# Splitting the first weight loads by use, k ahead of q in tiles 0 and 1, and w1, w3, w2 in more pieces

## The chip, the cores and the metric

One core of one Trainium2 chip runs the whole program. The metric is the device time of one execution in microseconds; the median of the runs counts.

## What is computed

A gated mix of a linear-attention block (a) and a gated feed-forward block (b), both of the same x (2048 tokens of 512, bf16). The reference, cut:

```
g = sigmoid((x * gate_w).sum(-1))
# a: 32 heads of 16
q, k, v = split(x @ wqkv)
pq, pk = phi(q), phi(k)          # phi(t) = where(t > 0, t + 1, exp(t)) + 1e-6
kv = einsum("bhsd,bhse->bhde", pk, v);  z = sum over s of pk
a = (pq @ kv) / (pq @ z + 1e-6) @ wo
# b: F = 1376
b = (silu(x @ w1) * (x @ w3)) @ w2
out = g * a + (1 - g) * b
```

## The kernel before

Tokens are cut into 16 tiles of 128 (`NT`), the model width 512 into four parts of 128 (`KC`, the index `kc`). The order of work on every engine is the order in which the program writes it; there is no planner. All loads are issued by one queue, SP's (`dq = nc.sync`), except for a small one (`touch`) on ACT's. Each DMA takes the next of eight semaphores in turn, and so an issue waits until the DMA eight places before it has landed.

**Loads** (L120 to L160). `x_first` brings the first two tiles of x into `xN` in natural layout. Then `load_wqk(kc)` (L126) brings four quarters of 256 KB, each with the rows of one kc and the columns of both q and k: `wqk[:, kc, :]`, of which `wq` is the first half of the columns and `wk` the second. After them come the DMA transposes that fill `xT` (x with the width on the partitions) for tiles 2 to 15 (L123), mixed with the natural loads of further tiles (L141), then the remainder columns `wr`, and the feed-forward weights `w1`, `w3` (one DMA each, L150), `wv`, `wo`, `w2` (one DMA, L154) and `w2x`.

**The first stage** (L372 to L419). Thirteen matmuls on a constant run while the loads are under way (L359). Tiles 0 and 1 of x are transposed by matmuls with an identity (L365) into PSUM banks, and copied to `xT` by DVE and ACT in turn (L379 to L382, L394). The projections of tiles 0 and 1, four accumulations (k and q of two tiles), go in the order of kc for the first two quarters, with k and q side by side (L183); then k's last two quarters, then q's. `phi` takes a finished accumulation through ACT's Exp (L196) and two DVE operations (L198, L201). `g_step(t)` multiplies xN's tile with pk's tile into the four banks 0 to 3, one for each kc, over all 16 tiles (L231). Banks 4 to 7 are handed out in turn by `mm_tile()`. Since `k_step(2)` takes bank 3 for its projection, the g_steps of tiles 0 and 1 do three banks first and the fourth later. From tile 2 on, each round of the loop is q of tile t, k of tile t + 2, g of tile t.

**Later stages.** The sum of pk over the tokens (`zacc`, on GpSimd), kv folded with wv and wo into `M2`, then for four blocks of 512 tokens the feed-forward (`glu_step`, L303 and L309), and for each tile the output (`out_step`, L475 and L492).

Of the kernel before, what the change touches and what calls it, by code (L numbers as in the profile page):

```python
# [8 lines left out]
ACT = mybir.ActivationFunctionType  # L9
# [7 lines left out]
def kernel(  # L17
# [17 lines left out]
    nc = tc.nc  # L35
    P = nc.NUM_PARTITIONS

    Bb, S, D = A_x.shape
# [3 lines left out]
    KC = D // P  # L42
    NT = S // P
# [3 lines left out]
    FC = F // P  # L47
# [14 lines left out]
    wqkv_r = A_wqkv.rearrange("(kc d) n -> d kc n", d=P)  # L62
    w1_r = B_w1.rearrange("(kc d) f -> d kc f", d=P)
    w3_r = B_w3.rearrange("(kc d) f -> d kc f", d=P)
# [15 lines left out]
        out=bmask[:], in_=bmask[:], pattern=[[-Dh, HPC], [0, Dh]], compare_op=ALU.is_ge,  # L80
# [3 lines left out]
        out=bmask[:], in_=bmask[:], pattern=[[Dh, HPC], [0, Dh]], compare_op=ALU.is_ge,  # L84
# [23 lines left out]
    wqk = consts.tile([P, KC, 2 * D], BF16, name="wqk")  # L108
    wq = wqk[:, :, 0:D]
    wk = wqk[:, :, D : 2 * D]  # L110
# [3 lines left out]
    w1 = consts.tile([P, KC, F0], BF16, name="w1")  # L114
    w3 = consts.tile([P, KC, F0], BF16, name="w3")
    w2 = consts.tile([P, FC, D], BF16, name="w2")
    xT = consts.tile([P, KC, S], BF16, name="xT")
    act_pre = consts.tile([P, 1], BF16, name="act_pre")
    dq = nc.sync
# [2 lines left out]
        ts = slice(t * P, (t + 1) * P)  # L122
        dq.dma_start(out=xT[:, :, ts], in_=x2d[ts, :], transpose=True)  # L123

    def load_wqk(kc):
        dq.dma_start(out=wqk[:, kc, :], in_=wqkv_r[:, kc, 0 : 2 * D])  # L126

    x_first = x2d[0 : 2 * P, :].rearrange("(p j) d -> p j d", j=2)
    dq.dma_start(out=xN[:, 0:2, :], in_=x_first)  # L129
# [1 line left out]

    touch = consts.tile([P, 2, 16], BF16, name="touch")
    nc.scalar.dma_start(out=touch[:], in_=wqkv_r[:, 1:3, 0:16])
    for kc in range(KC):
        load_wqk(kc)
    natural = {3: (2, 4), 5: (4, 8), 8: (8, 16)}
    for t in range(2, NT):
        load_xT(t)
# [3 lines left out]
    with nc.allow_non_contiguous_dma(reason="gate column"):  # L142
        dq.dma_start(
            out=wr[:, :, 2 * FR : NR], in_=gate_w.rearrange("(kc d o) -> d kc o", d=P, o=1)
        )
    dq.dma_start(out=wr[:, :, 0:FR], in_=w1_r[:, :, F0:F])
    dq.dma_start(out=wr[:, :, FR : 2 * FR], in_=w3_r[:, :, F0:F])
    for w, w_r, cuts in ((w1, w1_r, (0, KC)), (w3, w3_r, (0, KC))):
        for a, b in zip(cuts, cuts[1:]):
            dq.dma_start(out=w[:, a:b, :], in_=w_r[:, a:b, 0:F0])  # L150
    dq.dma_start(out=wv[:], in_=wqkv_r[:, :, 2 * D : 3 * D])
    dq.dma_start(out=wo[:], in_=A_wo.rearrange("(kc d) n -> d kc n", d=P))
    w2_r = B_w2[0:F0, :].rearrange("(fc f) d -> f fc d", f=P)
    dq.dma_start(out=w2[:], in_=w2_r)  # L154
    w2x_r = B_w2[F0:F, :].rearrange("(i r) d -> i (r d)", i=RP)
    dq.dma_start(
        out=w2x[:].rearrange("p r d -> p (r d)"),
        in_=w2x_r[None].to_broadcast([TPB, RP, RG * D]),
# [11 lines left out]
    bank = [psum.tile([P, D], FP32, name=f"bank{i}") for i in range(8)]  # L170
    turn = {"mm": 0, "ab": 0}

    def mm_tile():
        turn["mm"] += 1
        return bank[4 + (turn["mm"] - 1) % 4]
# [6 lines left out]
    def proj_mm(ps, t, w, kc):  # L182
        nc.tensor.matmul(  # L183
            ps[:], lhsT=xT[:, kc, t * P : (t + 1) * P], rhs=w[:, kc, :],
            start=(kc == 0), stop=(kc == KC - 1),
        )

    def project(t, w, ps=None):
        ps = mm_tile() if ps is None else ps
        for kc in range(KC):  # L190
            proj_mm(ps, t, w, kc)
        return ps

    def phi(ps, dst, name):
        e = work.tile([P, D], BF16, tag="e", bufs=4, name="e" + name)
        nc.scalar.activation(out=e[:], in_=ps[:], func=ACT.Exp)  # L196
        em = work.tile([P, D], BF16, tag="em", bufs=4, name="em" + name)
        nc.vector.tensor_scalar(  # L198
            out=em[:], in0=e[:], scalar1=1.0, scalar2=1e-6, op0=ALU.min, op1=ALU.add
        )  # L200
        nc.vector.scalar_tensor_tensor(  # L201
            out=dst, in0=ps[:], scalar=0.0, in1=em[:], op0=ALU.max, op1=ALU.add
        )
# [3 lines left out]
    def k_phi(t, ps):  # L207
        pk[t] = work.tile([P, D], BF16, tag="pk", bufs=5, name="pk")
        phi(ps, pk[t][:], "k")
        if t == 0:  # L210
            nc.gpsimd.tensor_copy(out=zacc[:], in_=pk[t][:])
        else:
            for i in range(ZP):
                cs = slice(i * D // ZP, (i + 1) * D // ZP)
                nc.gpsimd.tensor_tensor(  # L215
                    out=(zaccb if t == NT - 1 else zacc)[:, cs], in0=zacc[:, cs],
                    in1=pk[t][:, cs], op=ALU.add,
                )

    def k_step(t, ps=None):  # L220
        k_phi(t, project(t, wk, ps))

    def q_phi(t, ps):
        phi(ps, pq[:, t, :], "q")

    def q_step(t):
        q_phi(t, project(t, wq))

    def g_step(t, kcs=range(KC)):
        for kc in kcs:  # L230
            nc.tensor.matmul(  # L231
                bank[kc][:], lhsT=xN[:, t, kc * P : (kc + 1) * P], rhs=pk[t][:],
                start=(t == 0), stop=(t == NT - 1),
            )
# [128 lines left out]
    def transpose_block(t, kc, dst):  # L363

        nc.tensor.matmul(  # L365
            dst, lhsT=xN[:, t, kc * P : (kc + 1) * P], rhs=ident[:], start=True, stop=True
        )

    def transpose_kc(kc, ps):
        for t in range(2):  # L370
            transpose_block(t, kc, ps[:, t * P : (t + 1) * P])
# [3 lines left out]
    for t in range(2):  # L375
        transpose_block(t, 0, bank[t][:, 0:P])
    transpose_kc(1, bank[2])
    transpose_kc(2, bank[3])
    nc.vector.tensor_copy(out=xT[:, 0, 0:P], in_=bank[0][:, 0:P])  # L379
    nc.scalar.activation(out=xT[:, 0, P : 2 * P], in_=bank[1][:, 0:P], func=ACT.Copy)  # L380
    nc.vector.tensor_copy(out=xT[:, 1, 0 : 2 * P], in_=bank[2][:, 0 : 2 * P])
    nc.scalar.activation(out=xT[:, 2, 0 : 2 * P], in_=bank[3][:, 0 : 2 * P], func=ACT.Copy)  # L382
    first = {(t, n): mm_tile() for n, t in (("k", 0), ("k", 1), ("q", 0), ("q", 1))}
    w_of = {"k": wk, "q": wq}

    def first_mm(n, t, kc):
        proj_mm(first[t, n], t, w_of[n], kc)

    for kc in range(2):
        for n, t in (("k", 0), ("q", 0), ("k", 1), ("q", 1)):  # L390
            first_mm(n, t, kc)
        if kc == 0:
            transpose_kc(3, bank[0])
            nc.vector.tensor_copy(out=xT[:, 3, 0 : 2 * P], in_=bank[0][:, 0 : 2 * P])  # L394
    for kc in range(2, KC):
        for t in range(2):
            first_mm("k", t, kc)
    k_phi(0, first[0, "k"])
    k_phi(1, first[1, "k"])
    for kc in range(2, KC):  # L400
        first_mm("q", 0, kc)
    for kc in range(2, KC):
        first_mm("q", 1, kc)

    k_step(2, bank[3])
    q_phi(0, first[0, "q"])
    g_step(0, range(KC - 1))
    ps3 = project(3, wk)
    q_phi(1, first[1, "q"])
    k_phi(3, ps3)  # L410
    g_step(1, range(KC - 1))
    g_step(0, [KC - 1])
    g_step(1, [KC - 1])
    for t in range(2, NT):
        q_step(t)
        if t + 2 < NT:
            k_step(t + 2)
        g_step(t)


# [180 lines left out]
```

## Time and profile before

| | |
|---|---|
| median of 3 runs | 178.57 us (177.76 to 178.59) |
| the profiled execution | 178.0 us, of which 176.3 us span |
| granted TensorE clock | 1.0 |
| PE busy | 172.5 us, 98% of the span, 969 matmuls |
| DVE / ACT / POOL busy | 110.4 / 59.1 / 63.2 us |
| chain that ended last | PE 94%, DMA 2%, SP's queue 1% |
| HBM | 8.86 MB read, 2.10 MB written |
| DMA queue of SP | 28948 packets, 15.41 MB, 35.3% of 16 engines |

Times in the profile count from the start of the span. PE is TensorE's matmuls, PEld its weight loads, SPq SyncE's queue, which issues DMAs. A matmul's end is modelled, so that consecutive matmuls overlap in the records: what counts is the distance of their starts. The chain is followed back from the last instruction, at each step to what released it.

### The profile page before, as it was taken

Reading aid. Unit: us, or ns where it says so; the run is one execution under the profiler, and the core shown is the slowest. Engines: PE = TensorE matmul, PEld = TensorE weight load, DVE = VectorE, ACT = ScalarE, POOL = GpSimd, SP = SyncE. Lnnn points to the kernel's source line nnn. Section 1 sums busy time; section 2 is a strip of 40 time slices with the busy share of each in tenths; the row PEclk is TensorE's granted clock in tenths of the full one; section 3 lists DMA queues with packets and bytes.
Section 4 is the critical chain, followed back from the end, with each engine's and each line's share of the span. In section 5 each row is a group of like instructions: output and inputs, shape, how many; then the busy total and the mean of one; then the engine's idle time right before and its main releaser. Section 6 shows DMA issues by size and latency. Waiting matters only on the chain.

```text
span 176.3 us, 2685 instructions
## 1 busy us (share of the span) xinstructions
PE 172.5 (98%) x969; PEld 82.5 (47%) x969; DVE 110.4 (63%) x207; ACT 59.1 (34%) x109; POOL 63.2 (36%) x106
## 2 busy tenths in 40 slices
PE   8999999999999999999999999999999999999993
PEld 5444444444456443444444466444444444444453
DVE  1399788888764899777343477853435775344363
ACT  4354544544753443422423101134225123422000
POOL 5086657557300668486400044550000562000000
DMA  6998959995204111323200013330000233000001
GB/s 186 262 178 228 183 103 279 402 349 198 66 4 52 26 30 34 83 65 89 60 0 0 0 33 84 84 89 0 0 4 0 60 89 89 4 0 0 30 30 60
DMA packets 29232, 15.57 MB, mean 88 GB/s; under 512 B 21028, under 2 KB 27428, under 8 KB 29220
## 3 DMA queue, kind: packets, MB, share of 16 engines
q1 hardware_dynamic: 28948, 15.41, 35.3%
q8 instruction: 7, 0.11, 0.3%
q10 hardware_dynamic: 272, 0.01, 0.1%
q14 instruction: 5, 0.04, 0.1%
HBM read 8.86 MB, written 2.10 MB: 62 GB/s over the span
## 4 chain that ended last, share of the span: by engine, by line
PE 94%; DMA 2%; SPq 1%; DVE 0%; issue 0%
PE bank L492 20%; PE bank L303 20%; PE bank L309 20%; PE bank L183 15%; PE bank L231 8%; PE bank L475 8%; PE bank L245 3%; DMA wqk<-in_A_wqkv_dram 2%; PE bank L278 2%; SPq L126 1%; PE bank L447 0%; SPq L129 0%; PE bank L462 0%; DVE o L498 0%
## 5 line engine op out<-in xcount | busy, mean ns | idle before, releaser
L315 DVE TENSOR_TENSOR hT<-bank,sg 128x512 bf16<-128x512 f32 x40 | 27.3, 682 | 31.0 <-PE bank L309 30.9
L303 PE MATMUL bank<-xT,w 128*128 128x512 bf16 x160 | 41.1, 379 | 0.0
L309 PE MATMUL bank<-xT,w 128*128 128x512 bf16 x160 | 41.1, 379 | 0.0
L314 ACT ACTIVATE sg<-bank 128x512 bf16<-128x512 f32 x40 | 23.9, 597 | 45.9 <-PE bank L303 45.9
L492 PE MATMUL bank<-w,hT 128*128 128x512 bf16 (+2 forms) x180 | 37.5, 355 | 0.0
L337 POOL TENSOR_TENSOR pqs<-pq,rden 128x512 bf16<-128x512 bf16 x16 | 16.9, 1056 | 54.4 <-issue 46.9
L183 PE MATMUL bank<-wqk,xT 128*128 128x512 bf16 x128 | 30.8, 381 | 0.1
L215 POOL TENSOR_TENSOR zacc<-zacc,pk 128x128 f32<-128x128 f32 x56 | 23.3, 446 | 10.4 <-DVE pk L201 10.4
L492 PEld LDWEIGHTS <-hT 128*128 128x128 bf16 x180 | 16.7, 98 | 18.4 <-issue 0.8
L309 PEld LDWEIGHTS <-w 128*128 128x128 bf16 x160 | 15.7, 98 | 18.9
L303 PEld LDWEIGHTS <-w 128*128 128x128 bf16 x160 | 15.5, 98 | 18.2 <-issue 0.2
L498 DVE SCALAR_TENSOR_TENSOR o<-bank,omg_all,aga 128x512 bf16<-128x512 f32 (+2 forms) x18 | 12.5, 692 | 14.6 <-PE bank L492 11.7
L183 PEld LDWEIGHTS <-xT 128*128 128x128 bf16 x128 | 12.4, 98 | 15.2 <-issue 0.7
L322 POOL TENSOR_TENSOR pr<-pq,zb 128x512 f32<-128x512 bf16 x16 | 18.4, 1154 | 0.1
L231 PE MATMUL bank<-pk,xN 128*128 128x512 bf16 x64 | 16.4, 379 | 0.0
L475 PE MATMUL bank<-M,pqT 128*128 128x512 bf16 x64 | 16.1, 379 | 0.0
L196 ACT ACTIVATE eq<-bank 128x512 bf16<-128x512 f32 x16 | 9.4, 597 | 16.0 <-PE bank L183 16.0
L201 DVE SCALAR_TENSOR_TENSOR pk<-bank,emk 128x512 bf16<-128x512 f32 x16 | 11.1, 692 | 1.6
L196 ACT ACTIVATE ek<-bank 128x512 bf16<-128x512 f32 x16 | 9.4, 597 | 6.7 <-PE bank L183 6.7
L201 DVE SCALAR_TENSOR_TENSOR pq<-bank,emq 128x512 bf16<-128x512 f32 x16 | 11.1, 692 | 0.5
L326 DVE TENSOR_REDUCE den<-pr 128x32 f32<-128x512 f32 x16 | 10.8, 676 | 0.0
L231 PEld LDWEIGHTS <-xN 128*128 128x128 bf16 x64 | 6.3, 98 | 7.6
(54 smaller groups left out, 95.7 us busy)
## 6 DMA issues: line engine op xcount, KB each, us to landing
w<-in_B_w_dram SPq DMA_DIRECT2D x3, 1280.0 KB, 10.2
out_dram<-o SPq DMA_DIRECT2D x15, 128.0 KB, 1.9
wqk<-in_A_wqkv_dram SPq DMA_DIRECT2D x4, 256.0 KB, 3.7
xN<-in_A_x_dram SPq DMA_DIRECT2D x1, 1024.0 KB
xN<-in_A_x_dram SPq DMA_DIRECT2D x2, 256.0 KB, 2.8
xN<-in_A_x_dram SPq DMA_DIRECT2D x1, 512.0 KB, 4.7
wv<-in_A_wqkv_dram SPq DMA_DIRECT2D x1, 512.0 KB, 11.2
wo<-in_A_wo_dram SPq DMA_DIRECT2D x1, 512.0 KB, 12.1
```

What stands on the lines that cost most here:

```text
L183: nc.tensor.matmul(ps[:], lhsT=xT[:, kc, t * P : (t + 1) * P], rhs=w[:, kc, :], start=(kc == 0), stop=(kc == KC - 1),)
L196: nc.scalar.activation(out=e[:], in_=ps[:], func=ACT.Exp)
L201: nc.vector.scalar_tensor_tensor(out=dst, in0=ps[:], scalar=0.0, in1=em[:], op0=ALU.max, op1=ALU.add)
L215: nc.gpsimd.tensor_tensor(out=(zaccb if t == NT - 1 else zacc)[:, cs], in0=zacc[:, cs], in1=pk[t][:, cs], op=ALU.add,)
L231: nc.tensor.matmul(bank[kc][:], lhsT=xN[:, t, kc * P : (kc + 1) * P], rhs=pk[t][:], start=(t == 0), stop=(t == NT - 1),)
L303: nc.tensor.matmul(g_ps[:], lhsT=w1[:, kc, fs], rhs=xT[:, kc, tok], start=(kc == 0), stop=(kc == KC - 1),)
L309: nc.tensor.matmul(u_ps[:], lhsT=w3[:, kc, fs], rhs=xT[:, kc, tok], start=(kc == 0), stop=(kc == KC - 1),)
L314: nc.scalar.activation(out=sg[:], in_=g_ps[:], func=ACT.Silu)
L315: nc.vector.tensor_tensor(out=hT[tb][:, fc, :], in0=u_ps[:], in1=sg[:], op=ALU.mult)
L322: nc.gpsimd.tensor_tensor(out=pr[t][:], in0=pq[:, t, :], in1=zb[:], op=ALU.mult)
L475: nc.tensor.matmul(ps[:], lhsT=pqT[:, c, ts], rhs=M2[:, c, :], start=(c == 0), stop=(c == KC - 1),)
L492: nc.tensor.matmul(ps[:, 0 : cs.stop - cs.start], lhsT=hT[tb][:, fc, tt * P : (tt + 1) * P], rhs=w2[:, fc, cs], start=(fc == 0 and not sta ...
```

## The change

The first weights are loaded as wk quarter 0, wk quarter 1 (128 KB each), wk quarters 2 and 3 together, wq quarters 0 and 1 together, wq quarters 2 and 3 together (256 KB each): five DMAs in place of four. w1 and w3 are loaded in four DMAs each in place of one, w2 in two. In all that is eight DMAs more, 80 in place of 72.

The transposes of kc 2 and kc 3 of tiles 0 and 1 go between the projections: kc 2 behind k's first quarter and kc 3 behind its second. k of tiles 0 and 1 is finished in all four kc, then q, by halves. k_step(2) no longer uses bank 3 but the next bank of `mm_tile()`, and the g_steps of tiles 0 and 1 are whole. The loop now starts at tile 0.

```diff
-    def load_wqk(kc):
-        dq.dma_start(out=wqk[:, kc, :], in_=wqkv_r[:, kc, 0 : 2 * D])
+    def load_w(w, lo, hi):
+        cs = slice(D, 2 * D) if w is wk else slice(0, D)
+        dq.dma_start(out=w[:, lo:hi, :], in_=wqkv_r[:, lo:hi, cs])
...
-    for kc in range(KC):
-        load_wqk(kc)
+    for w, lo, hi in ((wk, 0, 1), (wk, 1, 2), (wk, 2, 4), (wq, 0, 2), (wq, 2, 4)):
+        load_w(w, lo, hi)
...
-    for w, w_r, cuts in ((w1, w1_r, (0, KC)), (w3, w3_r, (0, KC))):
+    for w, w_r, cuts in ((w1, w1_r, range(KC + 1)), (w3, w3_r, range(KC + 1))):
         for a, b in zip(cuts, cuts[1:]):
             dq.dma_start(out=w[:, a:b, :], in_=w_r[:, a:b, 0:F0])
...
-    dq.dma_start(out=w2[:], in_=w2_r)
+    for a, b in ((0, FC // 2), (FC // 2, FC)):
+        dq.dma_start(out=w2[:, a:b, :], in_=w2_r[:, a:b, :])
...
     transpose_kc(1, bank[2])
-    transpose_kc(2, bank[3])
     nc.vector.tensor_copy(out=xT[:, 0, 0:P], in_=bank[0][:, 0:P])
     nc.scalar.activation(out=xT[:, 0, P : 2 * P], in_=bank[1][:, 0:P], func=ACT.Copy)
     nc.vector.tensor_copy(out=xT[:, 1, 0 : 2 * P], in_=bank[2][:, 0 : 2 * P])
-    nc.scalar.activation(out=xT[:, 2, 0 : 2 * P], in_=bank[3][:, 0 : 2 * P], func=ACT.Copy)
-    first = {(t, n): mm_tile() for n, t in (("k", 0), ("k", 1), ("q", 0), ("q", 1))}
-    w_of = {"k": wk, "q": wq}
-
-    def first_mm(n, t, kc):
-        proj_mm(first[t, n], t, w_of[n], kc)
-
-    for kc in range(2):
-        for n, t in (("k", 0), ("q", 0), ("k", 1), ("q", 1)):
-            first_mm(n, t, kc)
+    ps_k = [mm_tile() for _ in range(2)]
+    for kc in range(KC):
+        for t in range(2):
+            proj_mm(ps_k[t], t, wk, kc)
         if kc == 0:
+            transpose_kc(2, bank[3])
+            nc.scalar.activation(
+                out=xT[:, 2, 0 : 2 * P], in_=bank[3][:, 0 : 2 * P], func=ACT.Copy
+            )
+        if kc == 1:
             transpose_kc(3, bank[0])
             nc.vector.tensor_copy(out=xT[:, 3, 0 : 2 * P], in_=bank[0][:, 0 : 2 * P])
-    for kc in range(2, KC):
+    k_phi(0, ps_k[0])
+    k_phi(1, ps_k[1])
+    ps_q = [mm_tile() for _ in range(2)]
+    for half in range(2):
         for t in range(2):
-            first_mm("k", t, kc)
-    k_phi(0, first[0, "k"])
-    k_phi(1, first[1, "k"])
-    for kc in range(2, KC):
-        first_mm("q", 0, kc)
-    for kc in range(2, KC):
-        first_mm("q", 1, kc)
-
-    k_step(2, bank[3])
-    q_phi(0, first[0, "q"])
-    g_step(0, range(KC - 1))
-    ps3 = project(3, wk)
-    q_phi(1, first[1, "q"])
-    k_phi(3, ps3)
-    g_step(1, range(KC - 1))
-    g_step(0, [KC - 1])
-    g_step(1, [KC - 1])
-    for t in range(2, NT):
-        q_step(t)
+            for kc in range(2 * half, 2 * half + 2):
+                proj_mm(ps_q[t], t, wq, kc)
+    q_phi(0, ps_q[0])
+    for t in range(NT):
+        if t > 1:
+            q_step(t)
         if t + 2 < NT:
             k_step(t + 2)
+        if t == 0:
+            q_phi(1, ps_q[1])
         g_step(t)
```

## The prediction, made before the changed kernel had run

> **What bounds the kernel now.** I read four views: the page's chain of work and busy times, the chain in order of time over the first 14 us, the timeline of the start, and the DMA answers for single loads. The page first.
>
> ```profile
> span 176.3 us, 2685 instructions
> PE 172.5 (98%) x969; PEld 82.5 (47%) x969; DVE 110.4 (63%) x207; ACT 59.1 (34%) x109; POOL 63.2 (36%) x106
> PE 94%; DMA 2%; SPq 1%; DVE 0%; issue 0%
> ```
>
> TensorE is the end-setter: 94% of the chain. The 2% of DMA is one piece, early. The chain over 0 to 14 us shows it:
>
> ```profile
> 1.25 0.42 SPq L126
> ...
> 2.66 4.38 DMA wqk<-in_A_wqkv_dram
> 7.04 0.04 issue
> 7.08 2.32 PE bank L183 x10
> 9.40 0.65 PE bank L231 x3
> ```
>
> The fourth quarter of wqk, issued at 2.66, lands at 7.04; the first matmul that needs it (k, kc 3, tile 0) starts at 7.08. From there the chain is PE without a break: ten matmuls in a row, then g_step, and so on to the end. I went through the starts of PE's matmuls after 7.08: a 512-column matmul follows another every 0.216 us, and what exceeds that is eight gaps of about 0.1 us, where the tiled matmuls of L278, L447 and L462 begin or end. The change touches none of these, so whatever it does to the time it does before about 13 us, while it delays no load past its use. The timeline there:
>
> ```profile
> 3.92 0.29 DVE L379 CAST xT<-bank 128x128 bf16<-128x128 f32 x1 [3.92 <-PE bank L365]
> 4.24 0.42 DVE L381 CAST xT<-bank 128x256 bf16<-128x256 f32 x1
> 4.26 1.26 PE L183 MATMUL bank<-wqk,xT 128*128 128x512 bf16 x4
> 4.45 0.38 ACT L382 ACTIVATE xT<-bank 128x256 bf16<-128x256 f32 x1
> 5.47 3.93 PE L183 MATMUL bank<-wqk,xT 128*128 128x512 bf16 x16
> 5.67 0.42 DVE L394 CAST xT<-bank 128x256 bf16<-128x256 f32 x1 [1.01 <-PE bank L365]
> 7.49 1.09 ACT L196 ACTIVATE ek<-bank 128x512 bf16<-128x512 f32 x2 [2.66 <-PE bank L183]
> 8.45 0.69 DVE L201 SCALAR_TENSOR_TENSOR pk<-bank,emk 128x512 bf16<-128x512 f32 x1
> 9.38 0.69 DVE L201 SCALAR_TENSOR_TENSOR pk<-bank,emk 128x512 bf16<-128x512 f32 x1
> ```
>
> The first projection matmul starts at 4.26, as soon as DVE's copy of xT (kc 0, tile 0) is done at 4.21. Ten of the sixteen matmuls of tiles 0 and 1 run before 7.08 and six after it: the sixteenth is done at 7.08 + 6 x 0.216 = 8.37, when k_step(2) begins. The only DMA wait in the whole PE stream is from 6.79 (the tenth, started at 6.58, has streamed) to 7.08: **0.29 us**.
>
> **The loads.** The four quarters of wqk (256 KB each, issued at 1.25, 1.72, 2.19 and 2.66) take 2.9, 3.2, 4.1 and 4.4 us, and so land at 4.12, 4.96, 6.32 and 7.04. After the change the same 1 MB goes as 128, 128, 256, 256 and 256 KB, k's half first. Two terms come with it. Rows of 2048 bytes become rows of 1024: in the trace's packet records a 2048-byte packet takes 84 ns and a 1024-byte one 46 ns, so each of the 16 DMA engines carries 64 x 46 = 2.94 us in place of 32 x 84 = 2.69, **+0.26 us** for the last byte. And SP issues one more DMA: 0.43 us (a wqk row) to 0.59 us (a two-row natural load). I count that at nothing for the weights, because the last quarter waits 4.4 us from issue with the engines busy all along; if that cover is gone it costs up to 0.59. By byte position: wk's first quarter about 3.8, its second about 4.2 to 4.5, its second half 4.96 + 0.13 = about 5.1, wq's first half 6.32 + 0.2 = 6.5, its second 7.04 + 0.3 = **7.35**. Bounds for the last: 6.9 (the last 2048-byte packet ends at 6.62, plus 0.26, no hold-up after it) to 8.9 (7.04 + 0.26 + 0.59 + one more stall like the longest packet of that stretch, 1.03). I take 7.35, nearest the quarter's own row.
>
> **PE's new order, step by step**, with the spacings of before (0.40 and 0.26 us for the two matmuls at 4.26 and 4.66, 0.216 later, 0.056 for a transpose). Four transposes in place of six run ahead of the copies; DVE's copy still ends at 4.21, so k kc 0 starts at 4.26 and 4.66. Transposes of kc 2 at 4.93, k kc 1 at 5.04 and 5.26, transposes of kc 3 at 5.47 and 5.53. k kc 2 could start at 5.58 but needs ACT's copy of the kc 2 block, which before lay hidden at 4.45: transpose done at 5.20, copy 0.38, about 5.68 (+0.10 new wait). k kc 3 needs DVE's copy: block done at 5.75, copy 0.42, 6.21 plus the 0.06 from copy to matmul: 6.26 and 6.48 (+0.15 new wait). So k of both tiles ends its stream at 6.69, and eight q matmuls follow: 6.69 + 8 x 0.2155 = **8.42**, if wq's first half is there by 6.65 (6.5 expected) and the second by 7.56 (7.35 expected). Against 8.37 that is **+0.05 us**. The 0.29 us wait for DMA is gone, and two waits for copies (0.25) plus the two transposes that formerly ran ahead of 4.26 (0.11) have taken its place, less some 0.03 of smaller gaps.
>
> **Who else waits.** k_step(2) used bank 3 and now takes the bank of k's tile 0, so it must wait for pk of tile 0. Before, from the start of that tile's last matmul (7.08) to the end of its pk (9.14) it was 2.06; now 6.26 + 2.06 + 0.06 = 8.38, just under 8.42: nothing. xT of tile 2 landed at 7.5 (issued 3.14, 4.4 us); moved by one issue and the slower weights it lands at 7.9 to 8.1, ahead of 8.42. xT of tile 3 is needed a k_step and a g_step later, at 10.15, two more us than the tile before it. The later transposes and natural loads come 0.5 to 0.7 us later: L183 of tile 4 is due at 12.7 and its xT landed at 10.1. k_step(4) takes the bank of q's tile 1, so pq of tile 1, the fifth phi on DVE, must be done by 12.74. Phis follow each other at 0.93 (8.45 to 9.38): 8.32 + 4 x 0.93 = 12.0, and 12.6 with two of the slow forms of L198 (0.56 in place of 0.29), as the same stage showed before; with all four slow 13.1, which costs +0.4. I take 0.
>
> **w1, w3, w2 in ten pieces in place of three.** Bytes and row lengths stay (2560 and 1024), so engine time stays; SP issues seven more at 0.43 to 0.58, 3.0 to 4.1 us. Queued behind them are wv, wo, w2x and zaT's transpose, which waits for GpSimd with SP idle for 9.6 us before it. w1 lands at 33.4 and w3 at 36.8 and their first use is at 46.1. Each piece waits for the DMA eight places earlier, all of them older and landed first. Cost 0; without that cover of 9 us it would be the 4 us.
>
> **Sum**: +0.05 us on the profiled 178.0 (span 176.3 and 1.7 around it). The plain runs have 178.57 as median; the same step on it gives 178.62.
>
> **The rivals.**
> *wq comes late (slower).* Its second half decides from 7.56 on, one for one. At the upper bound 8.9 it costs 1.36 + 0.05: 180.0; with one long stall alone, landing 8.4, 0.9: 179.5. For it: single packets of 0.6 to 1.03 us stand in the packet records between 4.1 and 5.2, and several of the engines stand still from about 6.1 to 6.8, when the xT transposes begin behind the weights. Against it: 7.04 already contains both.
> *A fixed price for each DMA (slower).* If a load costs its start and completion each time, and these do not overlap, the fifth piece adds one more. The least price for that in the rows is 2.6 us from issue to landing for xN less 1.0 until its first packet: about 1.6, so 7.04 + 1.6 = 8.64 and +1.1: 179.7. Against it: the four quarters land 0.72 to 1.36 apart, less than the 2.9 to 4.4 that each takes, so they overlap. The Trainium skill, "DMA: Bandwidth & Descriptors", sections "Anatomy of one DMA" and "Rules for kernel authors", speaks against this change: about 2 us fixed for each DMA, and under 64 KB mostly overhead, best at 1 MiB; by its 2.0 us an estimate of the time would be 178.6 + 1.5 = 180.1. The trace's overlap speaks against using it so.
> *The wait was larger than the profile shows (faster).* The median is 0.57 above the profiled run. If all of that was the last quarter landing later, PE waits 0.86 before and the new order, with 0.2 us of room for wq, keeps 178.0 + 0.05: 178.05. Faster by over 0.5% would take a wait of 0.9 more than the new one; nothing that PE does after 13 us leaves room for it.
>
> **How the numbers follow.** 0.5% is 0.89 us, about what a measurement of this kernel can tell from no change. Forecast (PE-paced start, 178.6): 0.53. Late wq: 0.22, past the bound. Fixed price: 0.09, past it. Larger wait before: 0.16, of which 0.08 past the bound (the plain runs spread from 177.76 to 178.59). So faster 0.08, same 0.53 + 0.08 = 0.61, slower 0.22 + 0.09 = 0.31. The range runs from 177.9 (most of the faster case, and a tenth below its 178.05) to 179.7 (the late wq up to one long stall and the milder fixed price); the forecast's own is 178.2 to 179.1, its upper end the 0.4 of slow DVE phis.
>
> **What would show it.** In the changed profile: first L185 matmul at 4.26; k kc 3 at about 6.3; the eight q matmuls without a gap from 6.7; k_step(2) at about 8.4; no DMA or a very small one in the chain after xN. The prediction is wrong if the chain names wqk with a landing after 7.6, if k_step(2) or k_step(4) waits for DVE by more than 0.3 us, or if any PE gap after 13 us is new.

## The result

The changed kernel takes 178.9 us (median of 9 runs, 178.69 to 179.13) against 178.32 for the kernel before (9 runs, 177.76 to 178.59): a ratio of 1.0032, 95% interval 1.0021 to 1.0044. It is slower by 0.58 us, a third of a per cent, inside the stated range and within 0.5%, but twelve times the +0.05 us of the sum. The profiled execution took 178.91 us. A ratio here weighs all fast runs, so where some of them stand apart it differs from the ratio of the two medians.

The page after, its span and the chain's shares:

```profile
span 177.2 us, 2675 instructions
...
PE 94%; DMA 3%; issue 1%; SPq 1%; DVE 0%
```

The chain over the first 14 us, in order of time (start, us, what):

```profile
...
2.19 4.46 DMA wqk<-in_A_wqkv_dram
6.65 0.04 issue
6.69 3.61 PE bank L185 x16
10.30 0.86 PE bank L233 x4
11.17 0.86 PE bank L185 x4
...
```

The wait is still for wqk, but for another load: wk's second half, issued at 2.19, lands at 6.65. The sixteen matmuls of the third line are four of k, eight of q and the four of k_step(2); twelve stand between the late load and k_step(2), so that this begins at 6.69 + 12 x 0.2155 = 9.28, and began at 8.37 in the profile before. The span differs by the same 0.9, so what follows k_step(2) takes as long as before. The medians differ by less, 0.58, because the profiled execution before was a quick one (178.0, with a median of 178.32) and the profiled execution after was not (178.91 and 178.9). The timeline of the start (start, us, what):

```profile
4.31 1.03 PE L185 MATMUL bank<-wqk,xT 128*128 128x512 bf16 x2
...
5.59 0.38 ACT L389 ACTIVATE xT<-bank 128x256 bf16<-128x256 f32 x1 [1.25 <-PE bank L367]
5.65 0.74 PE L185 MATMUL bank<-wqk,xT 128*128 128x512 bf16 x2
...
6.55 0.42 DVE L394 CAST xT<-bank 128x256 bf16<-128x256 f32 x1 [1.84 <-PE bank L367]
...
7.54 1.08 ACT L198 ACTIVATE ek<-bank 128x512 bf16<-128x512 f32 x2 [1.56 <-PE bank L185]
```

k's first two matmuls start on time, at 4.31. Those of kc 1 start at 5.65 in place of 5.04, on the landing of wk's second quarter at 5.61. Single DMAs, from issue to landing: the first quarter 2.8 us, the second 3.9, the half 4.5:

```profile
wqk<-in_A_wqkv_dram SPq DMA_DIRECT2D x1, 128.0 KB, 3.9
...
wqk<-in_A_wqkv_dram SPq DMA_DIRECT2D x1, 256.0 KB, 4.5
```

What the DMA engines did meanwhile stands in the table by stages. From 3.4 to 4.8 us (columns: PE, PEld, DVE, ACT, POOL busy, clock, share of the 16 DMA engines, GB/s), first the kernel before, then the changed one:

```profile
3.40:4.80 1.40, 1.40 (x10) 0.94 (x9) 0.72 (x2) 0.63 (x2) 0.00 (x0) 1.00 1.04 318
```

```profile
3.40:4.80 1.40, 1.33 (x8) 0.63 (x7) 0.72 (x2) 0.28 (x1) 0.00 (x0) 1.00 0.59 92
```

Before, the engines are full and move 318 GB/s. After, they are 59% busy, part of it in single packets of 0.6 to 0.8 us, and move 92. Several experiments ask what this rate has to do with the late landings.

### The profile page after: what moved, and what is told of

It reads as the page before. It is cut to its first block, busy times and chain, and to the rows that moved or that the text cites. A ratio compares the mean times of both kernels' runs of the same rounds, so it can differ in the third digit from the quotient of the medians.

```text
span 177.2 us, 2675 instructions
## 1 busy us (share of the span) xinstructions
PE 172.1 (97%) x952; PEld 82.6 (47%) x969; DVE 110.5 (62%) x207; ACT 59.3 (33%) x109; POOL 63.4 (36%) x106
## 4 chain that ended last, share of the span: by engine, by line
PE 94%; DMA 3%; issue 1%; SPq 1%; DVE 0%
PE bank L305 20%; PE bank L484 20%; PE bank L311 19%; PE bank L185 15%; PE bank L233 8%; PE bank L467 8%; PE bank L247 3%; DMA wqk<-in_A_wqkv_dram 3%; PE bank L280 2%; SPq L127 0%; PE bank L439 0%; SPq L130 0%; PE bank L454 0%; DVE o L490 0%
## 5 line engine op out<-in xcount | busy, mean ns | idle before, releaser
L305 PE MATMUL bank<-xT,w 128*128 128x512 bf16 x158 | 40.8, 379 | 0.2
L311 PE MATMUL bank<-xT,w 128*128 128x512 bf16 x156 | 40.5, 379 | 0.2
L484 PE MATMUL bank<-w,hT 128*128 128x512 bf16 (+2 forms) x176 | 37.0, 355 | 0.5 <-issue 0.3
L467 PE MATMUL bank<-M,pqT 128*128 128x512 bf16 x61 | 15.6, 379 | 0.1
```

Source lines behind the costliest of these rows:

```text
L305: nc.tensor.matmul(g_ps[:], lhsT=w1[:, kc, fs], rhs=xT[:, kc, tok], start=(kc == 0), stop=(kc == KC - 1),)
L311: nc.tensor.matmul(u_ps[:], lhsT=w3[:, kc, fs], rhs=xT[:, kc, tok], start=(kc == 0), stop=(kc == KC - 1),)
L467: nc.tensor.matmul(ps[:], lhsT=pqT[:, c, ts], rhs=M2[:, c, :], start=(c == 0), stop=(c == KC - 1),)
L484: nc.tensor.matmul(ps[:, 0 : cs.stop - cs.start], lhsT=hT[tb][:, fc, tt * P : (tt + 1) * P], rhs=w2[:, fc, cs], start=(fc == 0 and not sta ...
```

## The experiments

My theory after the result (theory 1): k of tiles 0 and 1 waits for wk's pieces, which come late, and too many matmuls stand behind them. Rivals: the pieces of w1, w3 and w2 cost the time (rival 2); the order is good and only the split is harmful (rival 3); TensorE reaches its full rate later (theory 4: matmuls of 512 columns start up to 0.427 us apart at first, and 0.216 apart from about 4.8 us on in the profile before). Each experiment was timed in five rounds beside the kernel before, so each has its own median of before.

**e1: only the pieces.**

```diff
-    for w, w_r, cuts in ((w1, w1_r, (0, KC)), (w3, w3_r, (0, KC))):
+    for w, w_r, cuts in ((w1, w1_r, range(KC + 1)), (w3, w3_r, range(KC + 1))):
...
+    for a, b in ((0, 2), (2, KC)):
+        dq.dma_start(out=wo[:, a:b, :], in_=wo_r[:, a:b, :])
...
-    dq.dma_start(out=w2[:], in_=w2_r)
+    for a, b in ((0, FC // 2), (FC // 2, FC)):
+        dq.dma_start(out=w2[:, a:b, :], in_=w2_r[:, a:b, :])
```

> The kernel before with w1, w3 and w2 in ten pieces (and wo in two, so that the DMAs number 80); first loads and first stage as before. Theory 1 (the slowdown of about 0.58 us comes from the first loads: wk's pieces land late, and k of tiles 0 and 1 waits for them): within 0.2 us of before, 178.3. Rival 2 (the many pieces hold up SP's queue or a later stage): 0.4 to 0.6 us slower, 178.8, with a new PE gap after 13 us.

Measured: 178.30 against 178.18, ratio 1.0005 (0.9991 to 1.0019). Eight more DMAs behind the first loads (wo, too, goes in two here) cost nothing that shows, at most 0.2%; rival 2 falls.

**e2: only the order.** The changed kernel with `load_wqk(kc)` for four whole quarters and with w1, w3, w2 whole.

> PE's new order (k of tiles 0 and 1 whole, then q) on the old loads, four quarters of 256 KB with k's and q's columns, and w1, w3, w2 whole. Theory 1: k of kc 3 needs the fourth quarter, which lands at about 7.04 as before, and ten matmuls (two of k, eight of q) stand behind it where six stood: k_step(2) at 7.08 + 0.43 + 1.73 = 9.24 and 0.87 us slower than before, 179.2. Rival 3 (the order is good and only the split is harmful): no slower than before, 178.3.

Measured: 179.05 against 178.18, +0.87 us, ratio 1.0056 (1.0034 to 1.0077). In its chain:

```profile
...
6.77 0.44 DVE xT L392
7.21 0.05 issue
7.25 3.20 PE bank L183 x14
...
```

Two matmuls of k, eight of q and four of k_step(2) start at 7.25; the fourth quarter had landed at 7.13 and the copy of the kc 3 block, now late on the path, ended at 7.21. The order alone loses no less than the whole change: it leaves ten matmuls behind the last load where the old one left six. Rival 3 falls. Whether the split of the loads wins back a part of this is not shown, since the intervals of this run and of the changed kernel overlap.

**e3: wk's first two quarters in one DMA.**

```diff
-    for w, lo, hi in ((wk, 0, 1), (wk, 1, 2), (wk, 2, 4), (wq, 0, 2), (wq, 2, 4)):
+    for w, lo, hi in ((wk, 0, 2), (wk, 2, 4), (wq, 0, 2), (wq, 2, 4)):
```

> The changed kernel with wk's first two quarters in one DMA of 256 KB in place of two of 128 KB (wo in two, so that the DMAs still number 80). Theory 1a (the gap in the loads between 3.4 and 4.8 us comes from small DMAs that the engines finish faster than the queue feeds them): wk's second half lands at about 5.3 to 5.8 in place of 6.65, and the time is 0.5 us under the changed kernel's, 178.4. Rival 1b (the gap comes from rows of 1024 bytes or from the first reads of wqkv, whatever the DMA's size): as the changed kernel, 178.9, wk's second half at 6.4 to 6.8.

Measured: 178.63 against 178.18, ratio 1.0023 (1.0007 to 1.0040). Its stage from 3.4 to 4.8:

```profile
3.40:4.80 1.40, 1.18 (x7) 0.55 (x6) 0.71 (x2) 0.28 (x1) 0.00 (x0) 1.00 1.07 294
```

The same bytes in the same rows of 1024 bytes, as one DMA, keep the engines full (294 GB/s), and the 256 KB land at 4.42, where the second of the two quarters landed at 5.61. So it is not the row length that starves them. But the half behind came at 6.78 in this profile, and not at the 5.3 to 5.8 that I expected:

```profile
...
1.73 5.05 DMA wqk<-in_A_wqkv_dram
6.78 0.04 issue
6.82 3.61 PE bank L187 x16
...
```

That is as late as in the changed kernel, with full engines. Summed from the packet records, 752 KB of x and weights had moved by 4.8 us and 973 KB by 5.6 (the changed kernel: 487 and 726; the kernel before: 864 and 1140). The half ends at 768 KB of the queue, so other loads' bytes behind it had moved well before it landed. Three single packets of 1.2 to 1.3 us, which start between 4.36 and 4.43, may have held it back; that is not shown. So a full rate is not enough for an early landing, and the pair of small DMAs is not the only thing that makes wk's half late. The run's interval overlaps with the changed kernel's. The rate behaved as theory 1a says, the landing did not.

**e4: whole quarters for kc 0 and 1, halves for kc 2 and 3, old order.**

```diff
-    for kc in range(KC):
+    for kc in range(2):
         load_wqk(kc)
+    for cs in (slice(D, 2 * D), slice(0, D)):
+        dq.dma_start(out=wqk[:, 2:KC, cs], in_=wqkv_r[:, 2:KC, cs])
```

> The kernel before with its own order, but the weights of kc 2 and 3 loaded as wk's half and then wq's half (256 KB each, rows of 1024 bytes); kc 0 and 1 as before. 72 DMAs. Theory 1: the wait of 0.29 us for the fourth quarter goes, since k of kc 2 and 3 is complete with the third DMA (about 6.4) and q's half is due at 7.2; time 0.1 to 0.3 us under before, 178.1. Rival 1b (rows of 1024 bytes cost the queue about 0.8 us): the third DMA lands at 7 or later, 0 to 0.6 us slower, 178.3 to 178.9.

Measured: 178.19 against 178.18, ratio 1.0000 (0.9984 to 1.0016). The third DMA landed at 6.14 and k of kc 3 no longer waited, but in this profile the first quarter came at 4.66 and the first matmul at 4.70. The 0.29 us that PE waited in the profile before was not to be had on the median. Two halves of 256 KB do no harm that shows either.

**e5: another early read.** `touch` over the first columns of wk in kc 1 to 3.

```diff
-    nc.scalar.dma_start(out=touch[:], in_=wqkv_r[:, 1:3, 0:16])
+    nc.scalar.dma_start(out=touch[:], in_=wqkv_r[:, 1:4, D : D + 16])
```

> The changed kernel, in which the small early read of wqkv on ACT's queue covers the first columns of wk in kc 1, 2 and 3 (before: the first columns of wq in kc 1 and 2). Theory 1c (wk's second quarter and second half are late because the first packets to their rows stall for 0.5 to 0.8 us): wk's second quarter lands before 5.0 in place of 5.61 and the time is 0.3 to 0.5 us under the changed kernel's 178.9 (about 0.1% over before). Rival (those stalls come whatever is read first): as the changed kernel, 0.3% over before.

Measured: 178.90 against 178.31, ratio 1.0032 (1.0018 to 1.0046); second quarter at 5.74, 104 GB/s from 3.4 to 4.8. Nothing changed in the loads: theory 1c falls. In this profile the half landed at 6.50, and then k of kc 3 waited for the copy of its block until 7.22, so here the late copy decided and not the load.

**e6: the transposes back where they were.** In the changed kernel, `transpose_kc(2, ...)` and its copy ahead of the projections, `transpose_kc(3, ...)` behind kc 0.

> The changed kernel with the transposes and copies of kc 2 and kc 3 where the kernel before has them (kc 2 ahead of the first projection, kc 3 behind kc 0). Theory 4 (TensorE reaches its full rate later, at 5.7 in place of 4.7 us, because the new order leaves it gaps early, and the copies stand on its path): full rate by about 5.0, k of kc 3 earlier, the time 0.2 to 0.4 us under the changed kernel's 178.9 (0.1 to 0.2% over before). Theory 1 alone (the loads decide): as the changed kernel, 0.3% over before, since wk's second half still lands at about 6.6.

Measured: 178.74 against 178.31, ratio 1.0022 (1.0009 to 1.0034). The second quarter still landed late, at 5.47, the half at 6.22, and the full rate came at about 6, not by 5.0: the place of the transposes is not what delays it. A little may be won by taking the copies off the path (0.1%, with overlapping intervals); the rest stays.

**e7: the same move in the kernel before.** Transposes and copy of kc 2 behind the four projections of kc 0.

> The kernel before with the transposes and the copy of kc 2 moved behind the four projections of kc 0, next to those of kc 3. Theory 4: the full rate comes about 1 us later than 4.7, and the last quarter is no longer what ends the wait: 0.2 to 0.4 us slower than before. Theory 1: the fourth quarter still lands at about 7.0 and the copies end before 6.8: within 0.1 us of before.

Measured: 178.36 against 178.31, ratio 1.0001 (0.9985 to 1.0016). In the old order the late transposes cost nothing; the fourth quarter landed at 7.10 and was still what k of kc 3 waited for. Nor did the full rate come later, but at about 4.9. So theory 4 falls as far as the transposes go; what a late full rate costs by itself this run does not test.

**e8: wk's second quarter on ACT's queue.**

```diff
-    nc.scalar.dma_start(out=touch[:], in_=wqkv_r[:, 1:3, 0:16])
+    nc.scalar.dma_start(out=wk[:, 1:2, :], in_=wqkv_r[:, 1:2, D : 2 * D])
-    for w, lo, hi in ((wk, 0, 1), (wk, 1, 2), (wk, 2, 4), (wq, 0, 2), (wq, 2, 4)):
+    for w, lo, hi in ((wk, 0, 1), (wk, 2, 4), (wq, 0, 2), (wq, 2, 4)):
```

> The changed kernel with wk's second quarter issued on ACT's queue at 0.86 us, in place of the small early read (wo in two, so that the DMAs still number 80). Theory 1a (the engines run out of descriptors between 3.4 and 4.8 us because SP issues the small loads too slowly): the second quarter lands by 4.3, the second half by 5.8, and the time is 0.3 to 0.5 us under the changed kernel's. Rival 1b/1c (stalls at first reads of wqkv): the second half still lands at 6.4 or later, 0.3% over before or more, since the early small read is gone.

Measured: 178.55 against 178.31, ratio 1.0019 (1.0003 to 1.0035).

```profile
3.40:4.80 1.40, 0.96 (x7) 0.36 (x6) 0.53 (x2) 0.28 (x1) 0.00 (x0) 1.00 1.15 351
```

The engines are full, 351 GB/s; the two quarters land at 4.14 (the one on ACT's queue) and 4.53, and the half at 5.38, over a microsecond earlier. k of kc 3 starts at 6.40, near the 6.3 that the prediction had. Then wq's first half comes at 7.18 and not at 6.5, and eight q matmuls stand behind that. xN came at 3.95 in place of 3.59.

**e9: the kernel before with only its first quarter cut in two** (and the harmless pieces of e1).

```diff
+    for cs in (slice(D, 2 * D), slice(0, D)):
+        dq.dma_start(out=wqk[:, 0, cs], in_=wqkv_r[:, 0, cs])
-    for kc in range(KC):
+    for kc in range(1, KC):
         load_wqk(kc)
```

> The kernel before, in its own order, with only the first quarter of wqk split into two DMAs of 128 KB, k's columns and q's (and w1, w3, w2 in pieces, which cost nothing in e1, so that the DMAs number 80). Theory 1a (two DMAs of 128 KB one behind the other on SP's queue leave the engines partly empty, whichever order PE has): q's half of the first quarter lands after 5.0 in place of 4.1 to 4.7, and the time is 0.4 to 0.8 us over before. Rival (the delay belongs to k's rows of kc 1, not to the size): the first 256 KB land by 4.7 and the time is within 0.2 us of before.

Measured: 178.99 against 178.37, ratio 1.0066 (1.0034 to 1.0098). Two DMAs of 128 KB in place of one of 256, and the old order loses as much as the whole change did: seven of the twelve runs lie between 178.55 and 179.07, and the other five, from 180.29 on, pull the ratio up. The profiled run (180.4) is one of the five. Stage and chain:

```profile
3.40:4.80 1.40, 1.40 (x9) 0.69 (x8) 0.72 (x2) 0.58 (x2) 0.00 (x0) 1.00 0.70 118
```

```profile
...
1.72 3.96 DMA wqk<-in_A_wqkv_dram
5.68 0.04 issue
5.72 1.44 PE bank L186 x3
7.16 0.21 PE bank L368 x2
7.37 4.41 PE bank L186 x16
...
```

118 GB/s, and q's half of kc 0 at 5.68, like wk's second quarter in the changed kernel. The rows are those of kc 0, so it isn't k's rows of kc 1. The last line is a second matter: sixteen matmuls that take 3.6 us elsewhere take 4.41, since PE still ran at half rate until about 9 (below).

**e10: the new order on the loads of e4**, with w1, w3 and w2 whole.

```diff
-    for w, lo, hi in ((wk, 0, 1), (wk, 1, 2), (wk, 2, 4), (wq, 0, 2), (wq, 2, 4)):
+    for kc in range(2):
+        dq.dma_start(out=wqk[:, kc, :], in_=wqkv_r[:, kc, 0 : 2 * D])
+    for w, lo, hi in ((wk, 2, 4), (wq, 2, 4)):
```

> PE's new order on the loads of e4 (kc 0 and 1 as whole quarters of 256 KB, then wk's half, then wq's half; 72 DMAs). Theory 5 (what the new order costs is the matmuls left behind wk's second half, twelve in place of six behind the last load): wk's half lands at about 6.2, k of kc 2 at 6.25 and 2.59 us more to k_step(2): 8.84, against 8.4 to 8.5 in the old order, 0.4 us over before (178.7). Rival 3 (with whole quarters first the new order costs nothing): as e4, equal to before.

Measured: 178.77 against 178.37, +0.40 us, ratio 1.0040 (1.0011 to 1.0070).

```profile
...
2.19 3.91 DMA wqk<-in_A_wqkv_dram
6.10 0.04 issue
6.15 3.62 PE bank L186 x16
...
```

With full engines (345 GB/s from 3.4 to 4.8) wk's half lands at 6.10, k of kc 2 starts at 6.15, and the same twelve matmuls stand behind it: k_step(2) at 8.74, 8.84 expected. On the same loads the old order (e4) equals the kernel before. So 0.40 us is the price of the order alone where the loads come well; two of the twelve runs, at 180.7 and 181.04, widen its interval.

**e11: the changed kernel once more**, unaltered.

> The changed kernel once more, beside the others on this chip. Theory 1: wk's second quarter lands after 5.3 and its second half after 6.1 again, 0.5 to 0.65 us over before. Rival (the late landings were one run's accident): second quarter by 4.9, and the time nearer to before.

Measured: 179.00 against 178.37, ratio 1.0041 (1.0028 to 1.0054). Second quarter at 5.69, half at 6.52, 78 GB/s: not one run's accident.

**e12: the first quarter cut by rows.**

```diff
-    for cs in (slice(D, 2 * D), slice(0, D)):
-        dq.dma_start(out=wqk[:, 0, cs], in_=wqkv_r[:, 0, cs])
+    for ps_ in (slice(0, P // 2), slice(P // 2, P)):
+        dq.dma_start(out=wqk[ps_, 0, :], in_=wqkv_r[ps_, 0, 0 : 2 * D])
```

> As e9, but the first quarter of wqk is cut across the partitions: two DMAs of 64 rows of 2048 bytes, 128 KB each, in place of two of 128 rows of 1024 bytes. If two DMAs of 128 KB on SP's queue are enough to let the engines run empty, the second lands after 5.0 and the time is 0.4 to 0.8 us over before, as in e9. If it takes twice the rows of half the length, the second lands by 4.7 and the time is within 0.2 us of before.

Measured: 180.56 against 178.27, ratio 1.0099 (1.0064 to 1.0135); the second piece landed at 5.25, 160 GB/s in the stage. Whole rows of 2048 bytes do not help: two DMAs of 128 KB, one behind the other on SP's queue, are enough to bring the rate down. SP's first three issues of weights also took 0.57 to 0.59 us each, in place of 0.41 to 0.43 in e9, so that the last quarter was issued 0.46 us later than there. The loss exceeds the expected 0.4 to 0.8 us because the twelve runs fall into two groups, four from 178.46 to 178.81 and eight from 180.16 to 181.38. The profiled one (178.7) belongs to the first, so what makes the second is not shown for this kernel.

## Why the prediction was right, and which of its terms were not

Right, as forecast: the time moved little, the outcome was decided early, and the time stayed inside the range. All fourteen profiles end 167.9 to 168.0 us after the start of k_step(2), whenever that is, so all that stands behind it took the same time in each. What sets that start differs (one execution each, us):

| profile | last wait before k_step(2), and its end | matmuls from there | k_step(2) | span |
|---|---|---|---|---|
| before | wqk's fourth quarter, 7.08 | 6 | 8.37 | 176.3 |
| e1 | the fourth quarter, 6.92 | 6 | 8.22 | 176.1 |
| e7 | the fourth quarter, 7.14 | 6 | 8.44 | 176.4 |
| e12 | the fourth quarter, 7.76 | 6 | 9.06 | 177.0 |
| e4 | the first quarter, 4.70 | 16 | 8.62 | 176.5 |
| e9 | the first quarter's second piece, 5.72 (then half rate until about 9) | 15 | 10.76 | 178.7 |
| after (the changed kernel) | wk's second half, 6.69 | 12 | 9.28 | 177.2 |
| e11 | wk's second half, 6.57 | 12 | 9.20 | 177.2 |
| e6 | wk's second half, 6.26 | 12 | 8.85 | 176.8 |
| e3 | wk's second half, 6.82 | 12 | 9.41 | 177.3 |
| e10 | wk's second half, 6.15 | 12 | 8.74 | 176.7 |
| e2 | DVE's copy of kc 3, 7.25 | 10 | 9.42 | 177.5 |
| e5 | DVE's copy of kc 3, 7.22 | 10 | 9.39 | 177.3 |
| e8 | wq's first half, 7.22 | 8 | 8.95 | 176.9 |

Also right: the pieces of w1, w3, w2 at nothing (e1); the first matmul at 4.26 (4.31); no wait for pk of tile 0 at k_step(2), none for pq of tile 1 at k_step(4). The eight q matmuls run without a gap, but not as forecast: wq's halves landed at 7.38 and 8.15, after the 6.65 and 7.56 by which they were needed, and were in time (for 7.55 and 8.41) only because k was later still. The rival that let the new order gain from a wait larger than 0.29 us before has e4 against it: with that wait gone the old order is no faster than the kernel before on the median.

Wrong: the sum, +0.05 us for +0.58, and with it the signs that were to show it (k of kc 3 at 7.12 and not 6.3, k_step(2) at 9.28 and not 8.4, a load in the chain). That the forecast of no change held is owed to the width of its 0.5%, in which a loss of 0.3% still fits, though the runs tell it from no change; it is luck as far as the mechanism goes.

The step that failed is the landing of wk's pieces "by byte position". I put the second quarter at 4.2 to 4.5 and the second half at about 5.1; in the two profiles of the kernel they came at 5.61 and 5.69, and at 6.65 and 6.52. The method took the rate of four DMAs of 256 KB for granted. With two of 128 KB at the head the engines moved 92 and 78 GB/s from 3.4 to 4.8, not 318; by 4.8 us the changed kernel had moved 487 KB in place of 864, about 1.2 us of transfer at 318 GB/s, which the rest of the stream inherited (wq's second half at 8.15 and 8.00 for 7.35). e9 shows this loss in the old order, e12 that the row length is not its cause, and e3 and e8 that one DMA of 256 KB, or two queues, fill the engines again. But the method fails without the pair too: in e3 the engines were full and wk's half still landed at 6.78. Only in e8 did it land near its place in the queue, at 5.38.

The rival that named a late load looked at the wrong one. It had wq's second half decide from 7.56 on. In truth wk's second half decided: it was due at 5.68, expected at 5.1 and came at 6.65. The rival of a fixed price for each DMA holds in part only: the loads do overlap in the queue, and eight more DMAs later on cost nothing, so there is no price for each; there is one for small DMAs one behind the other at the start. The Trainium skill, "DMA: Bandwidth & Descriptors", section "Rules for kernel authors", asks for small transfers to be coalesced and for at least 1 MiB in a DMA. That pointed the right way for 128 KB at the head of the queue (e9, e12) and had no effect for 320 KB further back (e1). The 2 us that the prediction tried as a price are, in the Trainium skill's section "Anatomy of one DMA" on the same page, a fit to DMAs that GpSimd issues; the loads here are issued by SP.

What the prediction had right in number but not in weight is the order. It counted the twelve matmuls behind wk's second half, four of k and eight of q, but took that load to be early, so that a late landing had no price. The old order has six behind 7.04 (1.29 us), the new one twelve behind 6.65 (2.59 us). With full engines that costs 0.40 us (e10); with the four old quarters 0.87 (e2). The new waits for copies, 0.25 in the sum, lay hidden under the later loads in the changed kernel's profiles, all but 0.04 us in e11; in e2 and e5 the copy of kc 3 decided. The spacings of before, which the sum used for the steps from 4.26 on, did not hold in the changed kernel either, where the full rate came at about 5.9; the later load hid that too.

Still open: why the engines run empty behind two small DMAs, and why wk's half was late in e3 without them. The packet records do not tell which engine carries which packet, and neither the early read (e5) nor the row length (e12) is it. How much of the 0.58 us is the split and how much the order is not settled: e3, e6 and e8, which take away one cause each, lie 0.24 to 0.45 us over the kernel before, and their intervals overlap with the changed kernel's. No experiment was faster than the kernel before, so there is no better version to show.

## What to carry to other kernels

Where a stage starts under its loads, count for each load the matmuls that stand behind it: the order that keeps work of every operand for the arriving quarter (k and q side by side) left six behind the last load, the order that finishes k first left ten to twelve. Do not assume that bytes arrive at the rate of the larger DMAs when the first ones are cut: look at the GB/s of that stage and at the landing of each load, which can be late at a full rate (e3), and cut the loads that have slack rather than the one that the first matmul waits for. Where a stage hands over to a dense rest, as here at k_step(2), the start of the rest tells in each profile what the stage cost.

## What the runs showed of the hardware that I had not expected

Two DMAs of 128 KB at the head of SP's queue, behind one of 256 KB, brought the rate from 3.4 to 4.8 us to 78 to 165 GB/s in six profiles (changed kernel twice, e5, e6, e9, e12); without such a pair on one queue it was 288 to 351 in eight (before, e1, e2, e3, e4, e7, e8, e10). The rate alone does not tell when a load lands: at 294 GB/s wk's half came at 6.78 (e3), at 92 GB/s at 6.65.

A late first load can cost more than its lateness. In e9's profiled run (180.4 us) one projection matmul started at 4.31 and the next, held by the load, at 5.72; from there on matmuls started up to 0.427 us apart until 8.88, and 0.216 apart from 9.24. In the profile before this change of pace came at about 4.8. The column of the granted clock reads 1.00 in both stretches, so the half rate is seen in the spacing alone. The Trainium skill, "TensorE: Matmul & The Clock Gate", section "What's actually happening", has the clock at half until an activity window of about 3.4 us has been busy. That e9 missed one such window is possible and not shown: some 4.3 us lie between the two changes, and in the other profiles the change came anywhere from 3.8 (e12) to between 6.4 and 6.8 (e3). Five of e9's twelve runs took 180.29 to 181.13; that all five have the late change is likely, but it is shown for the profiled one only. Runs above 180 us also stand in e2 (one of twelve), e10 (two) and e12 (eight), none of them profiled, and in none of the kernel before or of the changed kernel.
